# One attention block with a gated FFN on one core: the last output products gathered in two places of a step, row maxima sent two slots sooner, one set of differences computed earlier

## The chip, the cores and the metric

The kernel runs on one core of a Trainium2 chip. The metric is the device time of one execution in microseconds (us). Five engines work side by side, each through its own list of instructions in the order in which it was written: TensorE (PE in the profile; its weight loads are PEld), VectorE (DVE), ScalarE (ACT), GpSimd (POOL) and SyncE (SP, which here only starts transfers; ACT starts some too, and both are shown with a q behind the name when they do).

## What is computed

A transformer block over 2048 rows of width 512 with 32 heads of 16. A conditioning vector gives six modulation rows. The attention part is cut into 4 segments of 512 rows: inside a segment a causal softmax, across segments a running memory that is read with phi(q). The FFN has 1792 hidden columns.

```python
x = A_x
mod = (_silu(c) @ w_mod).reshape(c.shape[0], 6, 1, -1)
h = _layernorm(x) * (1 + ca) + sa
x = x + ga * A(h)                      # attention, below
h = _layernorm(x) * (1 + cb) + sb
return x + gb * (gelu(h @ B_w1 + B_b1) @ B_w2 + B_b2)

# A: for each segment s of 4
logits = einsum("bhqd,bhkd->bhqk", qs, ks) * scale + mask
a_dot = softmax(logits) @ vs
a_mem = (phi(qs) @ M) / (phi(qs) @ z + 1e-6)
o = g * a_mem + (1 - g) * a_dot        # g = sigmoid(beta) by head
M, z = M + phi(ks).T @ vs, z + sum(phi(ks))
...
return concat(o) @ wo
```

## The kernel before

**Stages.** The projections q, k, v and the memory come first (to about 188 us in the profile), then the attention steps (to about 470 us), then the FFN in two passes. The order on every engine is written out by hand; nothing reorders it.

**Attention steps.** The 128 pairs of segment and head are worked in 32 groups of four heads, numbered 0 to 31, eight to a segment, and each group as two pairs of heads. A group's q and k lie in a *stack* (tiles `qst`, `kst`, four of each in turn). There are two products for each head. The S products (`s_part`, lines 606 and 643 to 645) give logits with queries in rows; `masked_max` (line 613, DVE) takes each row's maximum. The T products (`st_part`, line 693) give the logits transposed, with the row maximum already subtracted: three extra rows of the stack hold it in bfloat16 pieces. So a group's T products wait for its maxima. S is run two groups ahead of T. The maxima's way is: DVE max, `m_rows` (two small POOL subtractions, line 661, tile `nm`), `m_put` (a PE transpose into the bank `pv`, line 667, then an ACT copy to `ms`, line 127), `m_send` (a 12 KB transfer from `ms` into the stack, line 675; SP starts it for groups 0 to 12, ACT from 13 on). ACT turns T products into weights (exponentials, lines 708 and 719), POOL zeroes the upper triangle (line 696), PE multiplies with V (line 733) into the same bank `pv`, which ACT copies out as `ts`.

**Slots.** One step of the program (function `block_kernel`, string `ORDER`) works the T products of group Q and the S products of group Q+2, cut into parts like `S1` or `T4`, with twenty slots `c0` to `c19` between them, into which all else is put. A position is 20 times the step plus the slot. `ORDER` begins

```python
'S1 c0 T2 T3 T2 c1 S2 c2 S3 T3 S3 c3 c4 c5 T5 S0 c6 c7 T0 c8 c9 '
```

The table `PRM` gives the positions. `mput` is the position of `m_put(Q)` from 20 Q; `m_send` follows one slot later. `wo` lists where the output product of a finished block of 128 rows, `wo_part` (line 821, four parts of three PE products into the bank `mm`), is put; one slot behind its last part follows `wo_out` (a DVE addition, line 839, for the last four blocks), six slots behind that its store to `X2D`. `ht` places four groups of transposes of the normalised rows of segment 0 (`ln2_turn`, line 574, an ACT activation behind each, line 576), for which POOL's four normalisations (line 568) must be done. `gate` places a 256 KB load of the last gate row into `gab`.

**FFN.** The first product is done for two row segments at once by a seven-product scheme: the inputs are sums and differences of quarters, `r_sub` (line 886) with the names t1 to t4, each split into a high and a low half (`r_hi` on ACT, `r_lo` on DVE, line 899). `step(n, i)` runs what `bg` has put into the i-th of seven places of round n. `ln2_turn` for segments 2 and 3 is put there too; its transposes go by turns into the banks `mm` and `spare`.

Of the kernel before, what the change touches and what calls it, by code (L numbers as in the profile page):

```python
# [28 lines left out]
 'pv': [[31, 0, 0, 512], [36, 1, 128, 512], [37, 2, 256, 512], [38, 3, 384, 512]],  # L29
 'pvlast': [[25, 0, 0, 512], [30, 1, 128, 512], [31, 3, 384, 512], [35, 2, 256, 512]],  # L30
 'mrows': -26,
 'mput': -17,
 'stacks': -65,
 'den': 95,
 'dnl': 18,
# [8 lines left out]
 'olo': 138,  # L44
 'quick': {'dnl': 11, 'den': 84, 'rbl': 12, 'mix': 107, 'ohi': 117, 'olo': 119},
 'end': {'dnl': 11, 'den': 84, 'rbl': 7, 'mix': 103, 'ohi': 111, 'olo': 116},
 'wo': [[20 * i + o for i in range(8) for o in (2, 5)]] * 2 + [[20 * i + o for i in range(4) for o in (2, 5, 8, 14)]],
 'wox': -25,
 'mixu': 12,
 'olou': 12,  # L50
 'ht': [502, 509, 516, 523],
 'ht1': 644,
 'ln': [{'in': [327, 367, 387, 407], 'stat': [418, 425, 437, 445], 'rstd': 449, 'on': [455, 475, 479, 495]},
        {'in': [527, 530, 547, 567], 'stat': [565, 577, 585, 597], 'rstd': 603, 'on': [624, 626, 628, 630]}],
 'wl': [26, 66, 77, 81],
 'gate': 197,
# [45 lines left out]
def block_kernel(ctx: ExitStack, tc: tile.TileContext, x, wq, wk, wv, wo, betaq, betam,  # L102
# [99 lines left out]
    with ExitStack() as pa:  # L202
# [124 lines left out]
        for ds in ((0,), (1, 2, 3)):  # L327
# [4 lines left out]
            n = slice(ds[0], ds[-1] + 1)  # L332
# [24 lines left out]
        rest = ((2, 3), (4, 5))  # L357
# [155 lines left out]
        for s in range(NSEG):  # L513
            for tok in PRM["A"][s].split():
                n = int(tok[1]) if len(tok) > 1 and tok[1].isdigit() else 0
# [64 lines left out]
    mm = psw.tile([128, 512], F32, name="mm")  # L580
# [3 lines left out]
    with ExitStack() as pb:  # L584
# [295 lines left out]
        def raw(p, n):  # L880
            return T2 if n == "t2" and p == 0 else hk(p, RAW.get(n, n))

        def r_sub(p, n, e=v):
            x, y = {"t1": ("b12", "b11"), "t2": ("b22", "t1"), "t3": ("b22", "b12"), "t4": ("b21", "t2")}[n]
            for o, i, j in zip(raw(p, n), raw(p, x), raw(p, y)):
                e.tensor_tensor(out=o, in0=i, in1=j, op=ALU.subtract)
# [6 lines left out]
        def r_hi(p, n, e=None):  # L893
            for k in range(2):
                copy(e or "a", R[n][0][k], raw(p, n)[k])
# [117 lines left out]
        for Q in range(-LEAD // 2, NP // 2 + 1):  # L1013
# [4 lines left out]
            for tok in ORDER.split():  # L1018
                n = int(tok[1:])
# [15 lines left out]
    def rest(U, *names):  # L1035
        for n in names:
            for x in [x for x in left if x[0] == n and x[1] == U]:
                left.remove(x)
                x[2]()

    with ExitStack() as pc:
# [6 lines left out]
        spare = pf.tile([128, 512], F32, name="spare")  # L1048
# [10 lines left out]
        def w_views(j, i):  # L1059
            t, lo, hi, src, o = WS[i]  # L1060
            x = (wb if src else wa)[j][:, o:o + hi - lo]
            return [z.rearrange("p a k n -> p (a k n)") for z in (wt1[t][j % 2][0][:, lo:hi], wt1[t][j % 2][1][:, lo:hi], x)]
# [5 lines left out]
        def w_lo(j, i):  # L1068
            h, l, x = w_views(j, i)
            v.tensor_tensor(out=l, in0=x, in1=h.bitcast(F32), op=ALU.subtract)  # L1070
# [24 lines left out]
        def bg(n, i, f, *a):  # L1095
            bgs.setdefault((n + i // 7, i % 7), []).append((f, a))
# [73 lines left out]
        r_lo(0, "t1")  # L1170
        r_hi(0, "t2")
        w_lo(0, 1)
        rest(15, "den", "rb_in")
        rest(14, "mem_mix")
        r_lo(0, "t2")
# [26 lines left out]
        for n in range(2 * FH):  # L1202
# [6 lines left out]
            if j + 1 < FH and n:  # L1209
                for i in range(7):  # L1210
                    bg(n, i, w_prep, n + 1, i)
        for n, i, f, *a in ((0, 0, rest, 14, "o_hi", "o_lo"), (0, 0, r_sub, 0, "t3"), (0, 0, r_sub, 0, "t4"), (0, 1, w_hi, 0, 2), (0, 1, w_hi, 0, 3),
                            (0, 3, r_hi, 0, "t3"), (0, 3, wo_late, 2, 3), (0, 3, r_lo, 0, "t3"), (0, 3, w_hi, 1, 0),
                            (0, 4, w_lo, 1, 0), (0, 4, w_lo, 0, 2), (0, 4, w_lo, 0, 3), (0, 4, load_w1, 2),
                            (0, 4, r_hi, 0, "t4"), (0, 4, rest, 15, "mix", "o_hi"), (0, 4, r_lo, 0, "t4"),
                            (0, 4, rest, 15, "o_lo"), (0, 5, g_out, 0, s1, s1, 0, 0), (0, 6, w_hi, 1, 1),
                            (2, 2, ln2_load, 2, 0), (2, 3, ln2_load, 2, 1), (2, 5, ln2_load, 2, 2), (2, 6, ln2_load, 2, 3),
                            (1, 0, w_lo, 1, 1), (1, 0, r_hi, 0, "b22"), (1, 1, wo_late, 3, 4),
                            (1, 1, w_hi, 1, 2), (1, 1, w_hi, 1, 3), (1, 1, r_lo, 0, "b22"), (1, 2, close_wo),
                            (1, 3, w_lo, 1, 2), (1, 3, w_lo, 1, 3)):  # L1220
            bg(n, i, f, *a)
# [14 lines left out]
        for s, n in ((2, 3), (3, 4)):  # L1236
            for b in range(4):
                bg(n, 1 + b, ln2_stats, s, b)
            bg(n, 5, ln2_rstd, s)
            for i in range(2):  # L1240
                bg(n, 8 + i, ln2_applies, s, 2 * i, 2 * i + 2)
            for d in range(KB):
                bg(n, 14 + d, ln2_turn, s, d, (mm, spare)[d % 2])

        w2r = {}

# [50 lines left out]
        for p in range(2):  # L1297
            n = FH * p + FH - 1
# [56 lines left out]
        for p in range(2):  # L1355
            for j in range(FH):
                quad(FH * p + j, j == 0)
            n = FH * p + FH - 1
# [3 lines left out]
            for m in range(NM):  # L1362
                s, f = 2 * p + m // FB, m % FB
# [68 lines left out]
```

## Time and profile before

| | |
|---|---|
| three runs | 785.25, 785.66, 789.05 us; median 785.66 |
| profiled execution | 784.93 us, its span 783.2 us |
| granted TensorE clock | 1.00 of full |
| PE busy | 764.9 us, 98% |
| DVE, ACT, POOL busy | 555.9, 472.4, 316.3 us (71, 60, 40%) |
| PE matmul records | 4549 |

The profiled execution is 0.73 us below the median and 1.7 us above its own span. PE is busy nearly throughout, so the table says little of what a change is worth; that is read from the places where PE stands still, and from what ended each of them. A busy PE is not a PE at its peak.

### The profile page before, as it was taken

To read this page: it belongs to the slowest core of one execution; us is meant where nothing else is said; L and a number is where in the kernel's file an instruction comes from. 1 tells how busy PE (TensorE), PEld (TensorE's weight loads), DVE (VectorE), ACT (ScalarE), POOL (GpSimd) and SP (SyncE) were. 2 spreads that over 40 slices of the span, in tenths; PEclk is the share of its full clock that TensorE was granted. 3 is DMA by queue.
4 is the path that set the end of the run, shared out by engine and by line. 5 is a ranking of instruction groups with operands and counts; after the bars stand their busy time and mean duration, and the time that the engine had idled before them with its cause. 6 is when DMAs were issued, how large, how long until landed. Compare 5 with 4: busy or idle time off the path is not lost.

```text
span 783.2 us, 14171 instructions
## 1 busy us (share of the span) xinstructions
PE 764.9 (98%) x4549; PEld 529.0 (68%) x4549; DVE 555.9 (71%) x1540; ACT 472.4 (60%) x910; POOL 316.3 (40%) x535
## 2 busy tenths in 40 slices
PE   9999999999999999999989999999999999999998
PEld 4877786877444445454445457787888888888887
DVE  6677677548989888888977898868569764432424
ACT  3465546364888877777768676766644446652221
POOL 1256458261468556665786671242000404200000
PEclk9999999999999999999999999999999999999999
DMA  9596956487465576768677755595666524545543
GB/s 337 185 295 228 317 179 221 166 275 258 139 187 166 175 207 190 212 205 243 185 188 210 222 156 166 184 309 177 202 240 208 184 95 162 172 148 166 173 126 116
DMA packets 108818, 156.09 MB, mean 199 GB/s; under 512 B 16324, under 2 KB 55620, under 8 KB 108744
## 3 DMA queue, kind: packets, MB, share of 16 engines
q1 hardware_dynamic: 106911, 153.39, 62.1%
q10 hardware_dynamic: 1833, 1.81, 0.7%
q8 instruction: 35, 0.57, 0.3%
q14 instruction: 39, 0.32, 0.1%
HBM read 93.95 MB, written 60.83 MB: 198 GB/s over the span
## 4 chain that ended last, share of the span: by engine, by line
PE 76%; DVE 8%; POOL 5%; DMA 4%; issue 4%; ACT 3%; ACTq 0%; SPq 0%; DVEq 0%; POOLq 0%
PE bx L1080 9%; PE att L693 6%; PE pv L733 6%; PE q L313 6%; PE bx L1349 6%; PE att L606 5%; PE by L1349 5%; PE bv L1349 5%; PE bv L1080 5%; PE k L313 4%; PE v L464 3%; PE mm L821 3%; DMA qst<-ms 3%; PE spare L1349 2%; PE by L1080 2%
## 5 line engine op out<-in xcount | busy, mean ns | idle before, releaser
L613 DVE CUSTOM_DVE_ANT_0 dump<-att,maskb 128x384 bf16<-128x384 f32 (+1 forms) x456 | 207.7, 512 | 36.2 <-PE att L606 17.9
L708 ACT ACTIVATE pt<-att 128x384 f32<-128x384 f32 (+1 forms) x256 | 125.6, 545 | 17.7 <-PE att L693 14.1
L696 POOL TENSOR_SCALAR_AFFINE_SELECT pt<-pt 128x256 f32<-128x256 f32 x256 | 105.5, 425 | 67.9 <-ACT pt L708 42.4
L693 PE MATMUL att<-qst,kst 99*128 99x256 bf16 (+3 forms) x512 | 107.7, 300 | 7.3 <-DMA qst<-ms 5.4
L606 PE MATMUL att<-kst,qst 96*128 96x384 bf16 (+1 forms) x456 | 103.9, 310 | 1.1 <-ACT pt L719 0.4
L693 PEld LDWEIGHTS <-kst 99*128 99x128 bf16 x512 | 43.8, 97 | 74.9 <-issue 37.7
L865 POOL TENSOR_TENSOR wb<-wa 128x256 f32<-128x256 f32 x24 | 20.1, 838 | 154.2 <-DMA wa<-in_w 123.1
L733 PE MATMUL pv<-pt,V 128*32 128x512 f32 (+1 forms) x992 | 79.8, 439 | 0.0
L719 ACT ACTIVATE pt<-att 128x256 f32<-128x256 f32 (+1 forms) x128 | 62.2, 494 | 27.8 <-PE att L693 15.4
L136 DVE TENSOR_TENSOR gl<-s,gh 128x512 fp32r<-128x512 f32 x34 | 24.1, 710 | 42.0 <-ACT gh L133 42.0
L606 PEld LDWEIGHTS <-qst 96*128 96x128 bf16 x456 | 37.9, 98 | 21.6 <-issue 14.2
L733 PEld LDWEIGHTS pv<-pt,V 128*32 128x32 f32 x992 | 25.8, 109 | 36.0 <-issue 30.4
L133 ACT ACTIVATE gh<-s 128x512 fp32r<-128x512 f32 x34 | 21.3, 628 | 46.8 <-PE spare L1349 18.7
L1085 ACT ACTIVATE s<-s,b1t 128x512 f32<-128x512 f32 x42 | 30.3, 722 | 21.3 <-DVE s L1089 21.1
L1089 DVE TENSOR_TENSOR s<-bv,s 128x512 f32<-128x512 f32 x28 | 19.2, 687 | 32.2 <-PE bv L1080 22.8
L613 DVE DVE_READ_ACCUMULATOR2_ANT nm<- 128x1 f32 x456 | 38.1, 84 | 0.0
L509 POOL TENSOR_TENSOR q<-qr,q 128x512 bf16<-128x512 f32 x16 | 18.7, 1167 | 27.7 <-ACT q L508 27.3
L500 POOL TENSOR_SCALAR qp<-qp 128x512 f32<-128x512 f32 x12 | 19.2, 1596 | 25.2 <-ACT qp L495 25.2
L136 DVE TENSOR_TENSOR w1ml<-s,w1mh 128x512 fp32r<-128x512 f32 x18 | 13.0, 721 | 21.6 <-ACT w1mh L133 21.6
L661 POOL TENSOR_TENSOR nm<-nm 128x16 f32<-128x16 f32 x64 | 13.9, 217 | 33.8 <-DVE nm L613 31.1
L133 ACT ACTIVATE w1mh<-s 128x512 fp32r<-128x512 f32 x18 | 11.3, 628 | 26.1 <-PE spare L1349 11.6
L313 PE MATMUL q<-Ahl,wqh 128*128 128x512 f32 x64 | 25.8, 404 | 0.2 <-DVE Ahl L136 0.2
(362 smaller groups left out, 2041.0 us busy)
## 6 DMA issues: line engine op xcount, KB each, us to landing
GD<-s SPq DMA_DIRECT2D x56, 256.0 KB
s<-GD SPq DMA_DIRECT2D x52, 256.0 KB
kst<-KD SPq DMA_DIRECT2D x32, 384.0 KB
qst<-QD SPq DMA_DIRECT2D x32, 384.0 KB
TD<-ts SPq DMA_DIRECT2D x32, 256.0 KB
xt<-X2D SPq DMA_DIRECT2D x28, 256.0 KB
wa<-in_w SPq DMA_DIRECT2D x28, 256.0 KB
QD<-q SPq DMA_DIRECT2D x16, 384.0 KB
```

The lines of the kernel that those rows point to most:

```text
L133: act.activation(hi, src, AF.Copy)
L136: lo_eng.tensor_tensor(out=lo, in0=src, in1=hi.bitcast(F32), op=ALU.subtract)
L313: pe.matmul(ps, a[:, k, 128 * g:128 * g + 128], b[k], start=(k == 0 and i == 0), stop=(k == KB - 1 and i == 2))
L606: pe.matmul(ps, q_of(P, h, i), k_of(P, h, 128 * (i + 1)), start=True, stop=True)
L613: v.tensor_tensor_reduce(out=dump[n_dump[0] % 2][:, :n], in0=src, in1=maskb[:, 512 - n:], scale=-1.0, scalar=-4 * NEG, op0=ALU.add, op1=AL ...
L693: pe.matmul(ps, k[:99, e, 128 * j:128 * j + 128], q[:99, e, 128 * j:512], start=True, stop=True)
L696: pool.affine_select(out=t, in_=t, pattern=pattern, compare_op=ALU.is_ge, fill=0.0, base=0, channel_multiplier=-1)
L708: act.activation(pt[:, h, :], ps[:, :n], AF.Exp, scale=0.25)
L719: act.activation(pt, pv_, AF.Exp, scale=0.25)
L733: pe.matmul(ps[32 * c:32 * c + 32, lo:hi], V[4 * s + j][:, VW * hd:VW * hd + 32], pt[:, c % 2, lo - o:hi - o], start=start, stop=stop)
L1080: pe.matmul(ps, a[:, i, k, :], b[k], start=start and k == 0 and c == 0, stop=k == 1 and c == 2, skip_group_check=not start)
L1349: pe.matmul(ps, a[:, c], w[:, lo:hi], start=(f == 0 and i == 0), stop=(last and i == 2))
```

## The change

Six things are edited.

1. `mput` goes from -17 to -19: `m_put` moves from slot c3 to slot c1 of the step before its group, `m_send` from c4 to c2, in all groups.
2. `wo` of segment 2 goes from slots 2, 5, 8, 14 to 2, 2, 5, 5 of steps 28 to 31. `wo_out` moves with it from c15 to c6, its store from position 21 to 12 of the step.
3. `ht`: each entry three slots later.
4. `gate`: from position 197 (step 9) to 209 (step 10).
5. `r_sub(0, "t3")` is called before `den` of block 15 instead of in the first place of FFN round 0.
6. `ln2_turn` of segment 2: at places 13, 15, 17, 19 instead of 14, 15, 16, 17, counted from round 3.

```diff
- 'mput': -17,
+ 'mput': -19,
- ... [[20 * i + o for i in range(4) for o in (2, 5, 8, 14)]],
+ ... [[20 * i + o for i in range(4) for o in (2, 2, 5, 5)]],
- 'ht': [502, 509, 516, 523],
+ 'ht': [505, 512, 519, 526],
- 'gate': 197,
+ 'gate': 209,
...
         w_lo(0, 1)
+        r_sub(0, "t3")
         rest(15, "den", "rb_in")
...
-        for n, i, f, *a in ((0, 0, rest, 14, "o_hi", "o_lo"), (0, 0, r_sub, 0, "t3"), (0, 0, r_sub, 0, "t4"), ...
+        for n, i, f, *a in ((0, 0, rest, 14, "o_hi", "o_lo"), (0, 0, r_sub, 0, "t4"), ...
...
             for d in range(KB):
-                bg(n, 14 + d, ln2_turn, s, d, (mm, spare)[d % 2])
+                bg(n, (13 + 2 * d) if s == 2 else 14 + d, ln2_turn, s, d, (mm, spare)[d % 2])
```

On PE, `m_put` of group 24 now stands right behind the third T product of its step (`att` with `qst` first is a T product, with `kst` first an S product, `pv` the bank that `m_put` writes):

```order
 L693 LDWEIGHTS kst3_2141
 L693 MATMUL att1_2063<-qst3_2140,kst3_2141 128x384
+L667 LDWEIGHTS nm0_2054
+L667 MATMUL pv0_2068<-identb_64,nm0_2054 128x128
 L606 LDWEIGHTS qst1_1837
 L606 MATMUL att2_2064<-kst1_1838,qst1_1837 128x256
```

Before, it stood behind six S products, one T product and one output product more:

```order
 L606 LDWEIGHTS qst1_1837
 L606 MATMUL att5_2067<-kst1_1838,qst1_1837 128x128
-L667 LDWEIGHTS nm0_2054
-L667 MATMUL pv0_2068<-identb_64,nm0_2054 128x128
 L821 MATMUL mm_2039<-woh_2052,oh7_4587 128x512
 L821 MATMUL mm_2039<-woh_2052,ol7_4602 128x512
```

What stood ahead of it now stands behind it in PE's list. On ACT, in the same step, the copy `ms` and the send (DMA) pass one exponential only, the fourth (`pt47_1`, second half):

```order
 L708 ACTIVATE pt46_1_4863<-att0_2062 128x384
 L708 ACTIVATE pt47_1_4869<-att1_2063 128x384
+L127 ACTIVATE ms24_4873<-pv0_2068 48x128
+L675 DMA qst0_1832<-ms24_4873 3x16x128
 L708 ACTIVATE pt47_1_4869<-att4_2066 128x384
-L127 ACTIVATE ms24_4892<-pv0_2068 48x128
-L675 DMA qst0_1832<-ms24_4892 3x16x128
 L719 ACTIVATE pt46_3_4898<-att0_2062 128x256
 L836 ACTIVATE xo1_1_4907<-mm_2039 128x512
```

So three exponentials still stand ahead of the copy. At the head of the FFN, DVE's list before has the differences of t3 (`hr1_0`, `hr1_1`) behind the work of blocks 14 and 15 (`dn`, `opk`, `ol`):

```order
L1070 TENSOR_TENSOR w1ml0_6081<-wb0_5837,w1mh0_6080 128x768
L775 RECIPROCAL dn15_6093<-dn15_6093 128x32
L776 TENSOR_SCALAR dn15_6093<-dn15_6093,omg_71 128x32
L899 TENSOR_TENSOR rt2l0_6063<-s40_6092,rt2h0_6061 128x512
L899 TENSOR_TENSOR rt2l1_6064<-s21_6090,rt2h1_6062 128x512
L793 TENSOR_TENSOR opk14_5933<-opk14_5933,rbB14_6041 128x512
L795 TENSOR_TENSOR opk14_5933<-opk14_5933,amB14_5935 128x512
L810 TENSOR_TENSOR ol14_6167<-opk14_5933,oh14_6165 128x512
L886 TENSOR_TENSOR hr1_0_6001<-hr1_2_6013,hr1_0_6001 128x512
L886 TENSOR_TENSOR hr1_1_6007<-hr1_3_6019,hr1_1_6007 128x512
```

In the changed kernel they come first:

```order
L1070 TENSOR_TENSOR w1ml0_6081<-wb0_5841,w1mh0_6080 128x768
L886 TENSOR_TENSOR hr1_0_6001<-hr1_2_6013,hr1_0_6001 128x512
L886 TENSOR_TENSOR hr1_1_6007<-hr1_3_6019,hr1_1_6007 128x512
L775 RECIPROCAL dn15_6093<-dn15_6093 128x32
L776 TENSOR_SCALAR dn15_6093<-dn15_6093,omg_71 128x32
```

Two instructions moved ahead of seven; the differences of t4 stay where they were.

More of the change, by code (lines that the diff above doesn't have):

```diff
@@ L46 @@
  'end': {'dnl': 11, 'den': 84, 'rbl': 7, 'mix': 103, 'ohi': 111, 'olo': 116},
- 'wo': [[20 * i + o for i in range(8) for o in (2, 5)]] * 2 + [[20 * i + o for i in range(4) for o in (2, 5, 8, 14)]],
+ 'wo': [[20 * i + o for i in range(8) for o in (2, 5)]] * 2 + [[20 * i + o for i in range(4) for o in (2, 2, 5, 5)]],
  'wox': -25,
@@ L1211, in block_kernel @@
                     bg(n, i, w_prep, n + 1, i)
-        for n, i, f, *a in ((0, 0, rest, 14, "o_hi", "o_lo"), (0, 0, r_sub, 0, "t3"), (0, 0, r_sub, 0, "t4"), (0, 1, w_hi, 0, 2), (0, 1, w_hi, 0, 3),
+        for n, i, f, *a in ((0, 0, rest, 14, "o_hi", "o_lo"), (0, 0, r_sub, 0, "t4"), (0, 1, w_hi, 0, 2), (0, 1, w_hi, 0, 3),
                             (0, 3, r_hi, 0, "t3"), (0, 3, wo_late, 2, 3), (0, 3, r_lo, 0, "t3"), (0, 3, w_hi, 1, 0),
```

## The prediction

> **What bounds the kernel now.** The page first: PE is busy in 98% of the span, and the transfers run at 199 GB/s.
>
> ```profile
> span 783.2 us, 14171 instructions
> PE 764.9 (98%) x4549; PEld 529.0 (68%) x4549; DVE 555.9 (71%) x1540; ACT 472.4 (60%) x910; POOL 316.3 (40%) x535
> DMA packets 108818, 156.09 MB, mean 199 GB/s; under 512 B 16324, under 2 KB 55620, under 8 KB 108744
> ```
>
> No product is added or removed, so all that can change is PE's idle time, 783.2 - 764.9 = 18.3 us. The list of waits for PE alone says who ended it (columns: total us, times, longest):
>
> ```profile
> PE att L693 <- DMA qst<-ms: 5.4, 6, 2.4
> PE bx L1080 <- DVE rt3l L899: 1.2, 1, 1.2
> PE mm L574 <- ACT hr L576: 0.7, 1, 0.7
> PE bv L821 <- DVE ol L810: 0.6, 1, 0.6
> PE att L574 <- POOL xt L568: 0.5, 1, 0.5
> ```
>
> The largest is T products that wait for their maxima's transfer, six times in 32 groups; then single waits at the head of the FFN and at the transposes. Each edit has one of these places, so I went through the timeline there, engine by engine. A row gives start, duration and, in brackets, the wait before it.
>
> **Maxima two slots sooner.** A group without a wait, 19, shows what the move is worth:
>
> ```profile
> 341.27 0.65 PE L693 MATMUL att<-qst,kst 99*128 99x384 bf16 x3
> 341.76 0.38 PE L606 MATMUL att<-kst,qst 96*128 96x256 bf16 x2
> 343.10 0.22 PE L667 MATMUL pv<-identb,nm 128*128 128x128 bf16 x1
> 344.47 0.81 PE L693 MATMUL att<-qst,kst 99*128 99x512 bf16 x4
> 341.07 0.60 ACT L127 ACTIVATE ts<-pv 128x512 f32<-128x512 f32 x1 [0.53 <-PE pv L733]
> 341.64 1.26 ACT L708 ACTIVATE pt<-att 128x384 f32<-128x384 f32 x3
> 343.57 0.26 ACT L127 ACTIVATE ms<-pv 48x128 bf16<-48x128 f32 x1
> ```
>
> The new slot is where the S products of 341.76 begin, so the transpose (line 667) goes 1.34 us sooner. `ts`, which frees the bank `pv` for it, ends at 341.67, 0.09 before the slot: just in time. But on ACT the copy `ms` passes only the fourth exponential, and the third ends at 342.90; so `ms` starts 343.57 - 342.90 = 0.67 us sooner, and the send too. Half of the 1.34 is lost there.
>
> Does a send 0.67 sooner land 0.67 sooner? Group 15 waits, group 16 does not:
>
> ```profile
> 303.82 0.32 SPq L175 DMA_DIRECT2D kst<-KD  x1
> ...
> 306.55 0.67 SPq L751 DMA_DIRECT2D TD<-ts  x1
> 308.08 0.73 ACTq L675 DMA_DIRECT2D qst<-ms  x1
> 315.07 0.66 PE L693 MATMUL att<-qst,kst 99*128 99x384 bf16 x3 [0.85 <-DMA qst<-ms]
> 317.65 0.73 ACTq L675 DMA_DIRECT2D qst<-ms  x1
> 323.63 0.65 PE L693 MATMUL att<-qst,kst 99*128 99x384 bf16 x3
> ```
>
> In group 15 two stack loads of 384 KB and three moves of 256 KB were started by SP between 303.82 and 306.55; these 1.57 MB take 7.9 us at 199 GB/s, and 12 KB sent by ACT at 308.08 are in use only at 315.07, 7.0 us later. Group 16 needs its data 5.98 us after the send and does not wait. So a send seems to land when what SP started ahead of it has drained. Nothing is started between 307.41 and 308.08, so I take nothing for group 15, and nothing for the two smallest waits (5.4 less the four quoted in this text leaves 0.6 for both); a gain of 0 to 1.3 us stays open. The Trainium skill (DMA: Bandwidth & Descriptors, Queues, rings and completion order) has it otherwise: each DMA engine takes turns between the queues of SP and ACT packet by packet, by which the 12 KB would not stand behind all of SP's backlog. That speaks for the rival below; the 7.0 us speak against it.
>
> Where POOL is late, the new slot makes PE wait, and all of PE's list behind it. Groups 24, 25 and 29:
>
> ```profile
> 385.29 0.38 PE L606 MATMUL att<-kst,qst 96*128 96x256 bf16 x2
> 385.93 0.51 POOL L661 TENSOR_TENSOR nm<-nm 128x16 f32<-128x16 f32 x2
> 404.47 0.66 PE L693 MATMUL att<-qst,kst 99*128 99x384 bf16 x3 [2.42 <-DMA qst<-ms]
> 433.46 0.38 PE L606 MATMUL att<-kst,qst 96*128 96x256 bf16 x2
> 435.35 0.23 PE L667 MATMUL pv<-identb,nm 128*128 128x128 bf16 x1
> 434.79 0.51 POOL L661 TENSOR_TENSOR nm<-nm 128x16 f32<-128x16 f32 x2
> ```
>
> Group 24: `nm` ends at 386.44, the slot is 385.29: a stop of 1.15 us where there was none. Group 25's wait of 2.42 can take that up, but its own send is then 1.15 later by PE and 0.67 sooner by ACT's list, so it and the T products at 404.47 come 0.5 later: +0.5 (0 if the backlog sets the landing, 1.15 if ACT gives nothing). Group 29: the slot is 433.46, `nm` ends at 435.30: 1.84, of which the 1.89 - 1.34 = 0.55 by which the transpose was late already are paid now; 1.3 more. A wait of 0.45 behind it goes:
>
> ```profile
> 444.16 0.66 PE L693 MATMUL att<-qst,kst 99*128 99x384 bf16 x3 [0.45 <-DVE cmv L562]
> ```
>
> So +0.85 there (0 to 1.3). Sum of this edit: +1.35 (0 to 2.45), and no gain but in rival A. The transfers that SP starts are not passed by ACT's sends except where the starts lie within 0.67 us of each other.
>
> **The gate load, the stores of segment 2.** Group 11's send stands behind `gab`, group 31's behind an `X2D` store:
>
> ```profile
> 272.17 0.45 SPq L989 DMA_DIRECT2D gab<-modD  x1
> 280.30 0.66 PE L693 MATMUL att<-qst,kst 99*128 99x384 bf16 x3 [1.02 <-DMA qst<-ms]
> 454.38 0.45 SPq L847 DMA_DIRECT2D X2D<-xb  x1
> 462.12 0.66 PE L693 MATMUL att<-qst,kst 99*128 99x384 bf16 x3 [0.48 <-DMA qst<-ms]
> ```
>
> Each is 256 KB, 1.3 us at 199 GB/s. The load goes behind the send (position 209 against 202), the store nine slots sooner, so both waits go: -1.0 and -0.5. In SP's list the sends of groups 0 to 12 pass no transfer but this load. Behind the send it can delay the next stack loads by 1.3 us (0 to 1.3); the list of waits shows none for stack loads, so I take 0. The store waits for DVE's addition, which is nine slots sooner as well.
>
> **Output products of segment 2.** The same products in other slots, no work more. The DVE addition of the last block passes two normalisations of segment 1, whose result PE's 16 transposes need at once:
>
> ```profile
> 468.88 1.16 DVE L568 TENSOR_SCALAR xt<-xt,cmv,crs 128x512 f32<-128x512 f32 x2
> 469.97 0.68 DVE L839 TENSOR_TENSOR xb<-mm,xb 128x512 f32<-128x512 f32 x1
> ```
>
> They end at 470.04, and the list has no PE wait for them. With the addition's 0.68 ahead of the last they end that much later: I take +0.5 (0, where PE is late itself or had room, to 0.68).
>
> **`ht`.** PE's wait of 0.5 for POOL's fourth normalisation is passed by the three slots: -0.5.
>
> **t3 sooner.** DVE at the hand-over to the FFN, and PE's wait:
>
> ```profile
> 480.14 0.35 DVE L775 RECIPROCAL dn<-dn 128x32 f32<-128x32 f32 x1 [1.27 <-DMA dn<-TD]
> 484.68 2.39 DVE L886 TENSOR_TENSOR hr<-hr,hr 128x512 f32<-128x512 f32 x2
> 487.00 1.28 DVE L886 TENSOR_TENSOR hr<-hr,s 128x512 f32<-128x512 f32 x2
> 489.53 0.50 PE L1080 MATMUL bx<-rt3l,w1mh 128*128 128x512 f32 x1 [1.21 <-DVE rt3l L899]
> ```
>
> The two differences take 1.28 us where POOL is still (the row of 487.00); DVE's idle 1.27 ahead of `dn` hides them. Behind, t4's two come to 484.68 and last up to 2.39, so `rt3l`, which follows, starts some 1.2 sooner: PE's 1.21 falls to about 0.1. -1.1. The wait for `ol` (0.6) is next and stays: DVE and PE have both moved by 1.1.
>
> **`ln2_turn` spread.** The third transposes waited 0.7 for ACT to empty `mm`; with two places between them the wait goes: -0.7. From there PE has no wait in the list, so it reaches the end.
>
> **The sum.** -1.0 - 0.5 - 0.5 - 1.1 - 0.7 = -3.8; +1.35 + 0.5 = +1.85; net -1.95. The profiled execution (784.93 us: span 783.2 and 1.7 around it, which stays) would come to 783.0. The median of the three runs shown, 785.66, is 0.73 above the profiled one; the forecast is on its scale: 785.66 - 1.95 = 783.7. With the open ends its own range is 782.2 to 785.3.
>
> **Rivals.**
> A. The transfer follows the send, and POOL is in time in the new slots since `ht` and `wo` have moved its neighbours. Group 15 gains 0.67, the two small waits 0.6, group 25 0.67, and the +1.35 vanish: 783.7 - 3.3 = 780.4. For it: the skill's rule. Against: group 15's 7.0 us; POOL's list ahead of `nm` in 24 and 29 is the same.
> B. ACT's send ends on the other side, slower. It now stands ahead of the fourth exponential, which frees a PSUM bank (six in turn) for the second of the four T products of 344.47, so about 344.7. Worked out: 342.90, 0.26 for `ms`, 0.73 for the send (as at 308.08) and 1.26 / 3 = 0.42 or a little more for the exponential: 344.3 to 344.4. A margin of 0.3 us; if ACT comes over 0.3 later, each of the 17 groups 13 to 29 pays the rest. At 0.5 late: 0.2 x 17 = 3.4, 787.1. Against: ACT is busy 60%.
> C. t3 does not help: `dn` of block 15 comes later than the data and with it the chain through `RD` to `ol`, so PE's 1.1 us turn up at `ol`: 784.8.
>
> **Chances.** Forecast 0.60, A 0.18, B 0.12, C 0.10. A measurement here tells about 0.5% from no change, 3.9 us: below 781.7 faster, above 789.6 slower. Faster: A and a tail of the forecast, 0.20; slower: B where ACT is 0.65 late or more, 0.05; within, 0.75. The range leaves out half of A and half of B: 781.0 to 787.0.
>
> **What would show it.** Right: no wait at group 11 and 31, `rt3l` and `mm` gone from PE's list; line 667 waiting for POOL in 24 and 29, by over 1 us each; `ms` sends 0.6 to 0.7 sooner from group 13 on. Wrong: group 15's T products no longer wait (A), T products waiting for ACT all through the groups (B), a wait for `ol` of over 1.5 us (C), or a new wait that none of these has.

## The result, and the profile after

| | before | after |
|---|---|---|
| median of 20 runs, side by side | 787.21 us | 787.6 us |
| ratio | | 1.0005, 95% interval 0.9988 to 1.0022 |
| profiled execution, its span | 784.93, 783.2 us | 788.42, 786.7 us |

No change that can be told from none: +0.4 us, between -0.9 and +1.7. Forecast were -1.95 us, which lies outside. (A change too small to be told was given 0.75, and that came out, though not for the reasons given.) In absolute terms 783.7 was 3.9 too low; 1.55 of that is the scale, since 20 runs put the kernel before at 787.21 and the three runs shown put it at 785.66. The other 2.35 us are the change. Single executions of one kernel spread over 1% and the two profiled ones are 3.5 apart, so below only ratios of many runs are read as times, and profiles are read for what stands where.

The page of the changed kernel:

```profile
span 786.7 us, 14171 instructions
PE 767.2 (98%) x4549; PEld 528.8 (67%) x4549; DVE 555.5 (71%) x1540; ACT 470.3 (60%) x910; POOL 315.2 (40%) x535
```

As many instructions as before on every engine. Of the 3.5 us between the two spans, 1.2 are idle time of PE (19.5 us against 18.3). The other 2.3 are PE busy for longer with the same 4549 products, which no wait explains: over the seventeen profiles of this case PE's busy time runs from 764.7 to 770.1 us. What the edits changed is who ends PE's idle time. The list of waits for PE alone (total us, times, longest):

```profile
PE pv L667 <- POOL nm L661: 4.0, 3, 2.2
PE att L574 <- DVE xt L568: 1.9, 2, 1.5
...
PE att L693 <- DMA qst<-ms: 1.4, 3, 0.8
PE bv L821 <- ACT oh L127: 1.3, 1, 1.3
...
PE bv L821 <- DVE ol L810: 0.9, 2, 0.6
PE bv L1080 <- DVE rb22l L899: 0.7, 1, 0.7
```

Set against the list of before: the maxima's transfers fell from 5.4 to 1.4, and `rt3l` (1.2), `mm` (0.7), POOL's `xt` (0.5) and DVE's `cmv` (0.5) are gone, 6.9 us in all. In their place stand 4.0 for `nm`, 1.9 for DVE's `xt`, 1.3 for `oh`, 0.3 more for `ol` and 0.7 for `rb22l`, 8.2 us. Nearly every wait that an edit aimed at went; about as much came.

**Line 667, groups 0, 24 and 29.** Group 0 before, in the timeline:

```profile
188.10 0.53 PE L464 MATMUL mm<-wvh,Ahh 128*128 128x512 f32 x1
188.98 0.51 POOL L661 TENSOR_TENSOR nm<-nm 128x16 f32<-128x16 f32 x2 [5.56 <-DVE nm L613]
191.71 0.22 PE L667 MATMUL pv<-identb,nm 128*128 128x128 bf16 x1
196.28 0.65 PE L693 MATMUL att<-qst,kst 99*128 99x384 bf16 x3
```

and after, with the same stop in groups 24 and 29:

```profile
189.66 0.51 POOL L661 TENSOR_TENSOR nm<-nm 128x16 f32<-128x16 f32 x2 [5.56 <-DVE nm L613]
190.23 0.23 PE L667 MATMUL pv<-identb,nm 128*128 128x128 bf16 x1 [1.14 <-POOL nm L661]
198.38 0.65 PE L693 MATMUL att<-qst,kst 99*128 99x384 bf16 x3
...
386.88 0.23 PE L667 MATMUL pv<-identb,nm 128*128 128x128 bf16 x1 [0.71 <-POOL nm L661]
404.48 0.66 PE L693 MATMUL att<-qst,kst 99*128 99x384 bf16 x3 [0.80 <-DMA qst<-ms]
435.36 0.23 PE L667 MATMUL pv<-identb,nm 128*128 128x128 bf16 x1 [2.17 <-POOL nm L661]
```

In group 0 the transpose had stood 2.2 us behind the end of `nm`; its new slot is ahead of the product of 188.10, and now PE reaches it 1.14 too soon. The T products of group 0 come 198.38 - 196.28 = 2.10 later, of which 189.66 - 188.98 = 0.68 was there before this place: 1.4 us lost. No wait of before stood here to be won.

**Transposes of segment 1**, the engines DVE and PE (`xb` is the addition of an output product):

```profile
468.92 0.62 DVE L568 TENSOR_SCALAR xt<-xt,cmv,crs 128x512 f32<-128x512 f32 x1
469.47 0.68 DVE L839 TENSOR_TENSOR xb<-mm,xb 128x512 f32<-128x512 f32 x1
...
470.67 0.68 DVE L793 TENSOR_TENSOR opk<-opk,rbB 128x512 f32<-128x512 f32 x1
...
471.45 0.69 DVE L795 TENSOR_TENSOR opk<-opk,amB 128x512 f32<-128x512 f32 x1
472.06 1.00 DVE L568 TENSOR_SCALAR xt<-xt,cmv,crs 128x512 f32<-128x512 f32 x2
...
472.65 0.33 PE L574 MATMUL att<-ident,xt 128*128 128x128 f32 x1 [1.52 <-DVE xt L568]
```

The addition (469.47) stands ahead of the second of four normalisations, and DVE as a whole is late: the last two end at 473.06, against 470.04 before. PE waits twice, 0.42 and 1.52 us.

**Head of the FFN.** The loads of block 14 in SP's queue, PE's first FFN product, and PE's wait for `oh` of block 14:

```profile
470.17 0.32 SPq L847 DMA_DIRECT2D X2D<-xb  x1
470.59 0.60 SPq L756 DMA_DIRECT2D dn<-TD  x1
...
481.52 0.60 SPq L788 DMA_DIRECT2D rbB<-RD  x1
482.56 0.39 PE L1080 MATMUL bx<-rb11h,w1mh 128*128 128x512 f32 x1
...
489.47 0.50 PE L821 MATMUL bv<-woh,oh 128*128 128x512 f32 x1 [1.30 <-ACT oh L127]
```

`rt3l` is in time, as forecast, but `oh`, which comes out of a chain of loads and work (`dn`, its move through `RD` to `rbB`, `opk`), is late: `rbB` starts 1.04 us ahead of the first FFN product, before (476.25 against 479.55) 3.30. SP's own list of waits says what stood ahead of `dn`: the store of segment 2's last block, which waits for the addition.

```profile
SPq L847 <- DVE xb L839: 6.6, 2, 6.4
```

### The profile page after: what moved, and what is told of

Same layout as the page of the kernel before. It is cut to its first block, busy times and chain, and to the rows that moved or that the text cites. A ratio compares the mean times of both kernels' runs of the same rounds, so it can differ in the third digit from the quotient of the medians.

```text
span 786.7 us, 14171 instructions
## 1 busy us (share of the span) xinstructions
PE 767.2 (98%) x4549; PEld 528.8 (67%) x4549; DVE 555.5 (71%) x1540; ACT 470.3 (60%) x910; POOL 315.2 (40%) x535
## 4 chain that ended last, share of the span: by engine, by line
PE 79%; DVE 6%; DMA 5%; issue 3%; ACT 3%; POOL 2%; ACTq 0%; SPq 0%; DVEq 0%; POOLq 0%
PE bx L1080 9%; PE pv L733 7%; PE att L693 7%; PE att L606 6%; PE q L313 6%; PE bx L1350 6%; PE by L1350 5%; PE bv L1350 5%; PE bv L1080 5%; PE k L313 4%; PE mm L821 3%; PE v L464 3%; PE spare L1350 2%; PE by L1080 2%; PE mm L1350 2%
## 5 line engine op out<-in xcount | busy, mean ns | idle before, releaser
L696 POOL TENSOR_SCALAR_AFFINE_SELECT pt<-pt 128x256 f32<-128x256 f32 x256 | 102.2, 414 | 68.7 <-ACT pt L708 54.0
L313 PE MATMUL q<-Ahh,wqh 128*128 128x512 f32 x64 | 26.1, 407 | 0.0
```

Source lines behind the costliest of these rows:

```text
L313: pe.matmul(ps, a[:, k, 128 * g:128 * g + 128], b[k], start=(k == 0 and i == 0), stop=(k == KB - 1 and i == 2))
L696: pool.affine_select(out=t, in_=t, pattern=pattern, compare_op=ALU.is_ge, fill=0.0, base=0, channel_multiplier=-1)
```

## The experiments

Ratios are to the kernel before, run beside each kernel; 0.1% is 0.79 us. "The changed kernel" stands at 1.0005.

### All maxima back

```diff
- 'mput': -19,
+ 'mput': -17,
```

> The changed kernel with the maxima's put and send where they were (-17); the other five edits stay. By the prediction's sum the move costs +1.35 us, so this kernel would be 1.35 faster than the changed one, 3.3 faster than before. Theory now, from the changed kernel's trace: the stops of PE at line 667 go (1.14 and 0.25 in groups 0 and 1, which the prediction left out, 0.71 in group 24, 2.17 in group 29: 4.3 together), and the waits of T products that the change had removed come back in groups 15, 17, 25 and 29 (0.85, 0.37, 1.6 of 2.42, 0.45: 3.3 together): about 1 us faster than the changed kernel. Rival: the move is worth what it was made for (T products no longer wait) and this kernel is slower than the changed one by 1 us or more. The waits behind segment 2 (1.9 at the transposes, 1.3 and 0.66 at the head of the FFN) stay in every case.

0.9956 (0.9931 to 0.9981), -3.5 us: 3.9 faster than the changed kernel. The prediction's sum for the other five edits was -3.3. Its list of waits:

```profile
PE att L693 <- DMA qst<-ms: 3.8, 4, 1.5
PE att L574 <- DVE xt L568: 1.9, 2, 1.5
...
PE bv L821 <- DVE ol L810: 0.6, 1, 0.6
```

No stop at line 667, and, which nobody had expected, no wait for `oh` and `rb22l`, though the store still stands ahead of `dn`.

### The maxima alone, on the kernel before

```diff
- 'mput': -17,
+ 'mput': -19,
```

> The kernel before with only the maxima's put and send two slots sooner. Prediction: +1.35 us (0 to 2.45), stops at line 667 in groups 24 (1.15) and 29 (1.84), none in group 0, and the wait of group 15 stays at about 0.85, since the send stands behind what SP started. Theory now: a stop of about 1.1 in group 0 as well, and the waits of groups 15 and 17 gone; net about +1. Rival (the transfer follows the send): group 15 gains its 0.67 in every case, the stops cost nothing in the end, and the time falls by 1 us or more.

1.0031 (1.0008 to 1.0053), +2.4 us.

```profile
PE pv L667 <- POOL nm L661: 4.1, 4, 2.0
PE att L693 <- DMA qst<-ms: 3.0, 4, 1.2
...
PE bv L821 <- ACT oh L127: 1.5, 1, 1.5
```

Stops of 1.14 (group 0), 0.28, 0.71 and 2.00, as in the changed kernel; group 15's wait fell to 0.06, group 17's did not (0.62). The wait for `oh` comes here too, without any edit to the store. The rival, a gain, is out.

### The last store later

```diff
-            if (s, b) >= (2, 3):
+            if s == 3:
...
-                if (s, b) < (2, 3):
+                if s < 3:
```

> The changed kernel with one edit: the store of segment 2's last block is put six slots behind its addition, as the other blocks' stores are, instead of right behind it. So SP no longer waits for DVE's addition (6.4 us in the changed kernel's list of SP's waits) ahead of the loads of dn and opk of block 14. Theory: these loads start about 3 us sooner (467.8 instead of 470.6), dn of block 14 is there when DVE asks, the whole chain dn, RD, rbB, dn of block 15, opk, oh comes 1.5 to 3 us sooner, and PE's new waits at the head of the FFN (1.30 for oh, 0.22 for ol, 0.66 for rb22l) go: 1.3 to 2.2 us faster than the changed kernel. The wait of 1.9 at the transposes stays. Rival (DVE itself is late, by its own list): the loads start sooner, but oh comes no sooner than 488.3 and the waits stay within 0.5.

0.9973 (0.9951 to 0.9995), 2.5 us faster than the changed kernel by the two ratios. The waits for `oh` and `rb22l` are gone, the 1.9 at the transposes stays. As the theory had it; but as the first experiment shows, the store is only one of the things that make this chain late: there `oh` is in time with the store where the change put it.

### The last block back

```diff
- ... for i in range(4) for o in (2, 2, 5, 5)]],
+ ... for i in range(3) for o in (2, 2, 5, 5)] + [62, 65, 68, 74]],
```

> The changed kernel with only the last block of segment 2 back at slots 2, 5, 8, 14 (so its addition stands behind the four normalisations of segment 1, and its store behind the loads of block 14); blocks 0 to 2 keep the two slots. Theory: the transposes' wait for DVE falls from 1.9 to 0.5 or less, and the head of the FFN loses its new waits (1.30, 0.22, 0.66): 2.5 to 3.5 us faster than the changed kernel, so 2 to 3 faster than before. Rival: the transposes wait because DVE is late by the three additions and the slow pair sums ahead of them, and the last block's place matters little: wait of over 1.2 stays, gain under 1.5.

0.9990 (0.9967 to 1.0013): 1.2 faster than the changed kernel, less than expected, though the waits fell as the theory said (0.5 at the transposes, none for `oh` and `rb22l`). One of 0.8 came at group 31's T products. The difference is uncertain by 2.3 us either way, which reaches to the expected 2.5.

### Five groups' maxima back

```diff
+            mput = -17 if Q in (0, 1, 2, 24, 29) else PRM["mput"]
...
-            ap(20 * Q + PRM["mput"], own, "pv", ("m", Q), m_put, (Q,), True)
-            ap(20 * Q + PRM["mput"] + PRM["msl"], m_send, Q)
+            ap(20 * Q + mput, own, "pv", ("m", Q), m_put, (Q,), True)
+            ap(20 * Q + mput + PRM["msl"], m_send, Q)
```

> The changed kernel with the put and send of groups 0, 1, 2, 24 and 29 back where they were; the other 27 groups keep the two slots. Theory (the move costs where POOL is not yet done, and only there): line 667 waits for POOL no longer (1.14, 0.25, 0.71, 2.17 go), and the FFN's head has its data in time again as with all maxima back; the time is that of the kernel with all maxima back, 3 to 4 us faster than the changed one, or up to 1 better than that, since waits like those of groups 15, 17 and 21 (0.3 to 1.5) stay away. Rival: the move costs all through the groups (ACT's send ahead of the fourth exponential, the transfers in another order), and then at least 1.5 us of the 3.5 to 3.9 that all maxima back brings are missing here.

0.9950 (0.9929 to 0.9971), level with all maxima back. So the cost of the move sits in these five groups, and the two slots in the other 27 are worth nothing that shows: 0.5 us, uncertain by 2.6 either way. The wait for `oh` is gone, but the head of the FFN is not wholly in time: one of 1.3 for `ol` stands there.

### All maxima and the last block back

Both edits above in one kernel.

> The changed kernel with both costly places undone: all maxima back at -17, and the last block of segment 2 back at 2, 5, 8, 14. Theory (the two costs add): the transposes' wait of 1.9 falls to 0.5 or less, as with the last block alone; 1.4 us faster than with the maxima alone back, so about 4.5 to 5 faster than before. Rival: the waits of T products at 365 and 401 us (1.5 and 1.2 with the maxima back) or the head of the FFN take it up again: no more than 0.5 faster than with the maxima alone back.

0.9942 (0.9920 to 0.9965), 1.1 faster than with the maxima alone back, -4.6 in all. The transposes' wait is 1.0, not 0.5, and group 25's is 2.4 here, against 1.2 with the maxima alone back.

### Stack loads behind the send

```diff
- 'stacks': -65,
+ 'stacks': -55,
```

> The kernel before with one edit: the stack loads of each group (384 KB twice) ten slots later, so that SP starts them just behind the send of the maxima of the group two earlier instead of 4 us ahead of it. No send is moved. Queue theory (a send lands when what SP started ahead of it has drained): 0.77 MB less stand ahead of each send, 3.9 us at 199 GB/s, so group 15's 7.0 us from send to use would need only about 3; T products wait for the maxima no longer in groups 15, 17, 21 and 25 (0.85, 0.37, 0.30, 2.42), 3 to 4 us of waits less, unless S products now wait for their stacks, which then shows in the list as waits of line 606. Rival (packets of the two queues take turns, the 12 KB are late for another reason): the waits on the maxima's transfer stay at about 5.4 in sum.

1.0277 (1.0246 to 1.0308), and not the test it was meant to be. The list:

```profile
PE att L606 <- DMA qst<-QD: 22.2, 17, 3.0
PE att L693 <- DMA qst<-ms: 4.0, 5, 1.4
```

S products now wait for their stacks, 17 times, and from group 13 on, where ACT sends, SP runs ahead of it, so that the loads still start 1 to 3 us before the send. But that moved them towards sends that had had less ahead of them. Group 16, which before needed no wait 5.98 us after its send:

```profile
335.92 0.38 SPq L175 DMA_DIRECT2D kst<-KD  x1
...
337.18 0.73 ACTq L675 DMA_DIRECT2D qst<-ms  x1
...
343.82 0.66 PE L693 MATMUL att<-qst,kst 99*128 99x384 bf16 x3 [0.50 <-DMA qst<-ms]
```

6.64 us from send to use. In the 1.26 us ahead of the send SP started both stack loads and the 256 KB of `rbB`, 1.05 MB; before, it started none of them there. The packets on the two queues say it directly, from the send on. `q1` is SP's queue, `q10` ACT's, whose 51 packets here are 48 of 256 B, the 12 KB, and three of 4 B; a row gives packets, MB and the share of the DMA engines' time. The first two rows are from the kernel before (317.65 to 319.31 us), the third from this one (337.18 to 342.50), the last two too (337.18 to 342.86):

```profile
q1 hardware_dynamic: 169, 0.27, 50.5%
q10 hardware_dynamic: 51, 0.01, 3.5%
...
q1 hardware_dynamic: 627, 1.53, 95.2%
...
q1 hardware_dynamic: 653, 1.57, 91.3%
q10 hardware_dynamic: 51, 0.01, 1.0%
```

Before, the 12 KB are through 1.7 us after the send, behind 0.27 MB of SP's. Here not one of their packets has started after 5.3 us and 1.53 MB of SP's, and they are through after 5.7 us. What stood ahead at the send (the sizes of all that SP had started, less its packets that had begun) was 0.28 MB before and 1.40 MB here. The same count for all 323 sends by ACT in the seventeen profiles: the last packet is never through before all but 0.1 MB of what stood ahead has gone, and in 224 of them it is through within 0.1 MB of that. So the queue theory's mechanism holds, and the waits of groups 15, 17, 21 and 25 are gone as it forecast. But their sum fell only to 4.0, since other groups now wait: 14, 16, 18 and 24, behind the moved loads, and 31.

### The products alone, on the kernel before

`wo` and `ht` as in the change, nothing else.

> The kernel before with only the output products of segment 2 in two places and the transposes of segment 0 three slots later. Prediction: -0.5 (group 31) + 0.5 (transposes of segment 1) - 0.5 (transposes of segment 0) = -0.5. Theory now: -0.5, +1.4 (the transposes' wait is 1.9, since the last addition passes three normalisations and two sums of block 14 and DVE is behind by then) and -0.5: +0.4, with the waits 0.42 and 1.52 at the transposes. Rival: the wait at the transposes was made by DVE's lateness from the other edits, and is 0.5 here.

1.0009 (0.9982 to 1.0035), too wide to tell -0.5 from +0.4. The transposes' wait is 1.4 with only this edit, so the products make it; group 31 waits 0.3 instead of 0.5, POOL's 0.5 at the first transposes is gone.

### The first three groups, and the two late ones, back

The line of the five groups with `(0, 1, 2)`, and with `(24, 29)`.

> The changed kernel with the put and send of groups 0, 1 and 2 alone back at -17. Theory: the stops of 1.14 and 0.25 at line 667 go, and with them the 1.4 to 2 us by which the T products of groups 0 to 2 came later than before; the stops of 0.7 and 2.2 in groups 24 and 29 and the late head of the FFN stay: 1.4 to 2 us faster than the changed kernel. Rival (what is lost early is caught up by a later wait, such as group 11's): no more than 0.5 faster.

> The changed kernel with the put and send of groups 24 and 29 alone back at -17. Theory: 0.7 and 2.2 of stops go, group 25's wait rises again from 0.8 to about 1.6 and group 29's T products wait 0.5 again (net 1.6), and the head of the FFN has oh in time as in the kernel with five groups back (1.3 to 1.5 less): 2.3 to 3 us faster than the changed kernel, so that with the 1.4 to 2 of the first three the 4.3 of all five are made up. Rival: the head of the FFN stays late (its wait of 1.3 for oh remains), since the order of the transfers comes from the other groups; then 1.6 at most.

0.9996 (0.9972 to 1.0020) and 0.9989 (0.9965 to 1.0013): 0.7 and 1.3 faster than the changed kernel, together 2.0 where all five brought 4.3. The wait for `oh` stays (1.5) with the first three back and is gone with the late ones back. Too coarse to share out the cost, so each was also moved alone on the kernel before (`mput = -19 if Q in (0, 1, 2)`, and `(24, 29)`):

> The kernel before with put and send of groups 0, 1 and 2 alone two slots sooner. Theory: line 667 waits 1.14 and 0.25 for POOL in groups 0 and 1, nothing there is won (their T products do not wait before), and nothing behind it takes it up: +1.4 us. Rival (taken up by a later wait such as group 11's or 25's): +0.3 or less.

> The kernel before with put and send of groups 24 and 29 alone two slots sooner. Prediction: stops of 1.15 and 1.84, net +1.35. Theory now: stops of about 0.7 and 2.0 at line 667, group 25's wait 2.42 falls by up to 0.7, group 29's 0.45 goes: +1.5; and dn of block 14 comes later, so that the head of the FFN waits 1.3 to 1.5 for oh in place of rt3l's 1.2: +1.5 to +2 in all. Rival (the head of the FFN is in time, as in the kernel with all of before): +1.5 or less and no wait for oh.

1.0036 (1.0011 to 1.0061) and 1.0023 (1.0001 to 1.0045): +2.8 and +1.8 us. Both cost by themselves, and the first three, which the prediction had not looked at, not less than the late two. (The profile of the first three alone is of an execution of 796.0 us, against a median of 788.7.)

### Five groups and the last block back

> The changed kernel with the five groups 0, 1, 2, 24 and 29 back at -17 and the last block of segment 2 back at 2, 5, 8, 14. Theory: the transposes' wait falls from 1.9 to 0.5 to 1.0; 1 to 1.5 us faster than with the five groups alone, about 0.993 to 0.994 of before, level with all maxima and the last block back (0.9942), since the two slots are worth at most 0.5 us in the other 27 groups. Rival (the two slots are worth their 0.67 us where a T product waits, as in groups 21 and 25): 1 us faster than that kernel.

0.9937 (0.9914 to 0.9960), -5.0 us: the best of all, level with the kernel that has all maxima back. The transposes' wait is 1.5 here, with the last block back; so that block's place does not make it alone. Its group 11 in the timeline:

```profile
272.67 0.78 SPq L675 DMA_DIRECT2D qst<-ms  x1
...
273.50 0.64 SPq L990 DMA_DIRECT2D gab<-modD  x1
...
279.96 0.66 PE L693 MATMUL att<-qst,kst 99*128 99x384 bf16 x3 [1.29 <-DMA qst<-ms]
```

The gate load is behind the send, and the wait is 1.29, more than the 1.02 of before.

### t3 back, from the kernel with maxima and last block back

```diff
-        r_sub(0, "t3")
         rest(15, "den", "rb_in")
...
+        ... (0, 0, r_sub, 0, "t3"), (0, 0, r_sub, 0, "t4"), ...
```

> All maxima back at -17, the last block of segment 2 back, and the differences of t3 back at their old place as well; what is left of the change is the gate load, two places for three blocks, the transposes of segment 0 and the spread at segment 2's second transposes. Prediction: t3 is worth 1.1 us, so this kernel is 1.1 slower than the same one with t3 moved (0.9942 of before), and PE waits 1.2 to 1.5 for rt3l again. Rival C of the prediction (the gain turns up at the next chain): the wait for rt3l comes back, but the wait for rb22l (0.65) goes, and the difference is 0.5 or less.

0.9973 (0.9951 to 0.9995), so t3 moved is worth 2.4 us there (0.9942 to 0.9973), uncertain by 2.5 either way, which holds the predicted 1.1. `rt3l` is waited for 1.1 again. Rival C's 0.5 or less is not excluded by the times alone.

### All output products back

The five groups back, and `wo` of segment 2 wholly as before.

> The changed kernel with groups 0, 1, 2, 24 and 29 back at -17 and all output products of segment 2 back at slots 2, 5, 8, 14. What is left of the change: two slots for 27 groups, the transposes of segment 0, the gate load, t3, the spread transposes of segment 2. Theory (the products' new place makes DVE late for the transposes of segment 1): their wait, 1.5 with only the last block back, falls to 0.5 or less, group 31's wait of about 0.5 comes back: 0.5 to 1 us faster than that kernel, 0.9927 or so of before. Rival (the wait there comes from how DVE and POOL happen to meet, not from the products): the wait stays at 1 or more and the time is the same or, with group 31's wait, 0.5 worse.

0.9948 (0.9928 to 0.9968), no faster than with the two places for three blocks. The transposes' wait is gone altogether, so the products do make it; but one of 1.05 stands at group 31's T products. The two places move a wait rather than remove one. All seventeen profiles agree: the transposes wait for DVE 1.4 to 1.9 us in the seven kernels with all four blocks in the new places, 0.2 to 1.5 in the four with three, and not at all in the six with none.

## Why the prediction was wrong

**The step that failed is the first term, the maxima: +1.35, measured +2.4 to +3.9.** Alone 2.4 (0.6 to 4.2); in company 3.9 (1.0005 against 0.9956; 1.5 to 6.2) and 3.8 (0.9990 against 0.9942; 1.2 to 6.3). Two of these three intervals still hold 1.35, so no single time shows the miss; what the term left out is seen in the traces. The mechanism was right, a stop at line 667 wherever POOL is behind the new slot, and in groups 24 and 29 it was sized well in sum (0.71 and 2.17 seen, 1.15 and 1.84 forecast). It was looked for in too few groups. The search began at places where PE waited before, and at late `nm` in the middle of the attention steps; groups 0 to 2 were put at nothing without being compared. In group 0 of the same profile `nm` ends at 189.49, 1.4 us behind the 188.10 at which the work behind the new slot begins; in groups 1 and 2 it is 0.3 and 0.2. The stops seen there are 1.14, 0.25 and 0.11: 1.4 us by the trace and +2.8 (0.9 to 4.8) by the runs of them alone, whose other 1.4 is not accounted for.

**"No gain but in rival A" was not refuted by any time, but the waits fell somewhat.** In one profile each, the waits for the maxima's transfer are 1.4, 3.0, 2.7 and 1.0 in the four kernels with all maxima sooner; 4.2, 2.5, 2.6, 3.7 and 2.5 in the five with 27 to 30 groups sooner, all six that had waited among them; and 5.4, 3.8, 4.1, 4.6 and 4.2 in five that send as before. On average that is 2.4 us less for all groups sooner and 1.3 for most, and part of it is no gain of the send. Where group 24 stops PE, group 25 waits 0.8 to 1.6, and without that stop, with its send as much sooner, 1.5 to 1.8. Group 15's wait is gone in the changed kernel, but also in six of the eight profiles in which that group sends as before. With the five groups back, 27 sooner groups gain nothing measurable. That sends stand behind what SP started ahead of them is shown by the packets (the experiment with the stack loads), and against it stands the rule quoted in the prediction from the Trainium skill (DMA: Bandwidth & Descriptors, Queues, rings and completion order), by which the two queues take turns: here 12 KB took 5.7 us behind 1.4 MB. Why the turns did not let them through sooner was not settled.

**Transposes of segment 1: +0.5, measured 1.4 to 1.9 of waiting.** The prediction costed the one addition that passes the normalisations (0.68) and took DVE's list to be otherwise in time. But DVE had no room. Before, PE began the 16 transposes, of which the first four read all four normalised blocks, at

```profile
469.79 1.97 PE L574 MATMUL att<-ident,xt 128*128 128x128 f32 x16
```

and the last normalisation ended 0.25 later, at 470.04. All four additions moved, each ahead of other work on DVE, and the last normalisation came 3.0 later, where PE came 0.3 later. With the products back the wait is zero.

**The head of the FFN: t3's -1.1 and `ln2_turn`'s -0.7 came, and 2.1 came beside them.** The wait for `mm` is gone in every kernel that has this edit, and stands (0.5 to 0.9) in those that lack it. That for `rt3l` is 0.3 or less in the ten kernels with t3 moved, and 1.1 to 1.5 in six of the seven without; in the seventh, the maxima alone, PE waits 1.5 for `oh` instead. But `oh` of block 14 had little to spare before:

```profile
483.41 0.63 ACT L127 ACTIVATE oh<-opk 128x512 fp32r<-128x512 f32 x1 [1.64 <-DVE opk L795]
...
484.99 0.39 PE L821 MATMUL bv<-woh,oh 128*128 128x512 f32 x1
```

0.95 us, and its chain begins with a load in SP's queue. "The store waits for DVE's addition, which is nine slots sooner as well" named the wait and not what is queued behind it: the loads of block 14. In the first experiment, with the same store but later maxima, the chain holds:

```profile
466.42 0.32 SPq L847 DMA_DIRECT2D X2D<-xb  x1
466.84 0.60 SPq L756 DMA_DIRECT2D dn<-TD  x1
...
476.05 0.60 SPq L788 DMA_DIRECT2D rbB<-RD  x1
...
480.34 0.39 PE L1080 MATMUL bx<-rb11h,w1mh 128*128 128x512 f32 x1
```

`rbB` starts 4.29 us ahead of the first FFN product, not 1.04; from the load of `dn` to `rbB` the chain takes 9.2 us here and 10.9 in the changed kernel. The same two rows sort all seventeen profiles: where `rbB` starts less than 2.7 us ahead, PE waits for `oh` (0.3 to 1.5, in six kernels), where more, it does not (eleven kernels; in one of these, with 2.8, it waits 1.3 for `ol`). Why the sooner maxima make this chain slower is not shown. It is not the store alone: of the six kernels with the wait for `oh`, four have the store as before.

**The gate load: -1.0, not run by itself.** Group 11's wait fell from 1.02 to 0.31 in the changed kernel. Over all it is 0.0 to 1.3 in the eleven kernels with the load behind the send, 0.7 in the middle one; of the six with the load ahead, it is 0.6, 0.9, 1.0 and 1.0 in four, 2.9 in that with the first three groups moved and none in that with the stack loads moved. So perhaps 0.3 came, less than the spread. What had been read as the cause was not the only one. **Group 31: -0.5 held.** With the last block in its new place group 31's T products do not wait in five kernels and wait 0.2 and 0.3 in two; in the ten with the block in its old place they wait 0.4 to 1.3 in nine.

**Rivals.** A was wrong on POOL being in time, and the packets speak against it on the transfers. B, ACT late at the fourth exponential all through the groups, did not happen: waits of T products for ACT are 0.2 us in the changed kernel, and where nothing waits (group 19) the send stands 6.78 us ahead of the T products instead of 5.98, 0.8 sooner where 0.67 was forecast. C's sign, a wait for `ol` of over 1.5 us, came nowhere (1.3 at most). The wait for `oh` is not C: it comes without t3 moved as well (1.5 with the maxima alone).

**The sum.** -1.95, and 1.4 for groups 0 and 1, 1.4 for the transposes, 2.1 at the head of the FFN (2.82 after against 2.56 before, where -1.8 was forecast) and 0.3 for the gate load; less 1.2 for the waits of groups 15 and 17 that went unforeseen, and 0.5 because groups 24, 25 and 29 together came out at 0.8. That gives +1.5 for these two profiles, in which PE's idle time grew by 1.2; measured are +0.4 (-0.9 to +1.7). "All that can change is PE's idle time" did not hold from one profile to the next, as the 2.3 us of busy time show. Nor do the forecast's open ends, added up straight, give its own range of 782.2 to 785.3: 0 to 2.45 for the maxima with a gain of up to 1.3, 0 to 0.68 for the transposes and 0 to 1.3 for the stack loads make 780.5 to 786.3, and on that scale the measured +0.4 is 786.1. The other five edits together came to the forecast (-3.5, forecast -3.3), but not by its terms: transposes and gate load alone miss by some 2 us in these profiles, and what made that up is not shown.

## What to carry to other kernels

When an instruction is moved ahead by a fixed number of slots in all of many groups, compare its input's end with the new slot in every group, the first ones of a ramp-up above all, and not only where a wait is seen; here five of 32 groups cost more than the other 27 gained. When a store is moved, read what stands behind it in its queue, to the end of that chain, and how much that chain has to spare. A wait for a transfer behind a backlog, read from one profile, varies by a microsecond from kernel to kernel: a term that rests on one such row deserves a range from zero.

## What the runs showed of the hardware

A 12 KB transfer started by ACT becomes late by what SP started ahead of it: group 16's was through 1.7 us after the send with 0.28 MB of SP's still to go, and 5.7 us after it with 1.40 MB; in none of 323 such sends was the last packet through before all but 0.1 MB of what SP had started ahead of it. And ten slots' delay of loads that had landed in time cost 2.8%, 22 us of waits, although no byte was added.
